# A retention layer with channel mixing: q in packets of two tokens, and the decay moved from the q/k product to v and y

## The chip, the cores and the metric

One core of a Trainium2 chip. The metric is the device time of one execution in microseconds; the profile's "span" (first to last instruction) is about 2 us shorter than the timed run. Executions on a single core are sorted into "fast" and "slow" by their time alone: an execution over 1.5% above the fastest of the same kernel is called slow.

## The reference, cut to what matters

```
# attention: q, k, v are (4 batches, 8 heads, 768 tokens, 64), float32
gamma = 1 - 2 ** (-5 - arange(8))                # one decay per head
state = gamma * state + outer(k[t], v[t])        # per head, 64 x 64
y[t]  = q[t] @ state / 8

# channel mix: x = y with heads side by side, (4, 768, 512)
x_prev = x shifted by one token
xk = mu_k * x + (1 - mu_k) * x_prev ;  xr likewise with mu_r
out = sigmoid(xr @ w_r) * (relu(xk @ w_k) ** 2 @ w_v)     # w_k 512x1024, w_v 1024x512, w_r 512x512
```

## The kernel before

The kernel works on chunks of 128 tokens, 24 in all. Inside a chunk the recurrence is a masked product (k columns by q columns, then by v); between chunks a 64 x 64 state per head is carried. The decay is folded into q and k as they are cast to float16: q gets gamma^u / 8, k gets gamma^-u. A small planner inside the program simulates the engines, orders all tasks, and puts "fillers" (matmuls on a tile of zeros) where it expects TensorE to wait. The parts that the change touches:

```python
# loads: 128 tokens on 128 partitions, 8 heads x 64 values each: packets of 256 bytes
src = s[b, :, c * C : (c + 1) * C, :].rearrange("h t d -> t h d")
nc.sync.dma_start(out=t32.tile[:, n], in_=src)                    # k, q, v in turn
# weights: one transfer into 128 partitions each, rows of 2 KB
wkd = moe_w_k.rearrange("(co ci) f -> ci co f", ci=P)             # w_k in two halves; w_r, w_v alike
# cast of q and k with the decay: VectorE, 24 of them
nc.vector.tensor_tensor(out=qks.tile, in0=t32.tile[:, 0:2],
    in1=Gqk[par].unsqueeze(3).broadcast_to([P, 2, H, D]), op=ALU.mult)
# cast of v: GpSimd or ScalarE
nc.gpsimd.tensor_copy(out=v16.tile, in_=t32.tile[:, 2])
# y leaves PSUM: ScalarE or VectorE
nc.scalar.copy(out=x_out(), in_=y())
... (transposes, masks, state, channel mix, the planner: cut)
```

## Time and profile before

| | before |
|---|---|
| time, median | 181.09 us (4 runs, 180.81 to 181.51), beside the changed kernel |
| span | 178.9 us |
| TensorE / VectorE / ScalarE / GpSimd busy | 167.7 / 150.8 / 102.7 / 29.8 us |
| fillers | 153 |
| second-layer product (w_v) starts | 30.49 us |

The prediction below shows the page and reads it. Three things more are needed for the comparison. First, the page's row of GB/s, in 40 slices of 4.5 us each:

```profile
GB/s 111 223 339 304 253 386 244 222 226 204 255 256 232 200 177 166 136 225 167 199 217 230 191 190 257 194 214 234 31 59 62 0 117 4 59 60 4 117 59 59
```

Second, VectorE's timeline at three casts of weights (start, duration, line, and in brackets how long the engine stood idle and what ended it):

```profile
17.29 1.22 DVE L347 CAST wk<-wk 128x2048 f16<-128x2048 f32 x1
24.54 1.22 DVE L347 CAST wr<-wr 128x2048 f16<-128x2048 f32 x1
30.30 1.23 DVE L347 CAST wv<-wv 128x2048 f16<-128x2048 f32 x1 [2.21 <-DMA wv<-in_moe_w_v_dram]
```

Third, TensorE's timeline at its start:

```profile
1.12 5.07 PE L269 MATMUL pm<-warm 128*128 128x256 f16 x30 [1.12 <-DVE xT L484]
7.18 0.62 PE L398 MATMUL px<-c_sb,qks 128*128 128x128 f16 x8 [0.99 <-DVE qks L385]
7.64 0.71 PE L269 MATMUL pm<-warm 128*128 128x256 f16 x5
```

Thirty fillers in a row take 5.07 us, the first ones at half rate, and by the first transposes TensorE is quick.

### The profile page before, as it was taken

To read this page: it belongs to the slowest core of one execution; us is meant where nothing else is said; L and a number is where in the kernel's file an instruction comes from. 1 tells how busy PE (TensorE), PEld (TensorE's weight loads), DVE (VectorE), ACT (ScalarE), POOL (GpSimd) and SP (SyncE) were. 2 spreads that over 40 slices of the span, in tenths; PEclk is the share of its full clock that TensorE was granted. 3 is DMA by queue.
4 is the path that set the end of the run, shared out by engine and by line. 5 is a ranking of instruction groups with operands and counts; after the bars stand their busy time and mean duration, and the time that the engine had idled before them with its cause. 6 is when DMAs were issued, how large, how long until landed. Compare 5 with 4: busy or idle time off the path is not lost.

```text
span 178.9 us, 4138 instructions
## 1 busy us (share of the span) xinstructions
PE 167.7 (94%) x1698; PEld 113.5 (63%) x1698; DVE 150.8 (84%) x269; ACT 102.7 (57%) x162; POOL 29.8 (17%) x37
## 2 busy tenths in 40 slices
PE   7799899989999799999999999999999999999971
PEld 5678685565877475856757657567666486576450
DVE  0568995988899999999999999999999987999111
ACT  2123565265774866881857936949618458284560
POOL 0030202042130101320131223115213212010000
PEclk9999999999999999999999999999999999999999
DMA  4999999999999878597898889889111030110311
GB/s 111 223 339 304 253 386 244 222 226 204 255 256 232 200 177 166 136 225 167 199 217 230 191 190 257 194 214 234 31 59 62 0 117 4 59 60 4 117 59 59
DMA packets 81298, 30.77 MB, mean 172 GB/s; under 512 B 75512, under 2 KB 75648, under 8 KB 81280
## 3 DMA queue, kind: packets, MB, share of 16 engines
q1 hardware_dynamic: 81280, 30.51, 70.6%
q8 instruction: 13, 0.21, 0.5%
q14 instruction: 5, 0.04, 0.1%
HBM read 24.22 MB, written 6.29 MB: 171 GB/s over the span
## 4 chain that ended last, share of the span: by engine, by line
PE 61%; DVE 14%; SPq 10%; DMA 6%; ACT 3%; issue 3%; POOL 2%; DVEq 0%
PE pm L579 18%; PE pm L543 17%; PE pm L572 9%; SPq L373 6%; DMA wv<-in_moe_w_v_dram 6%; PE px L398 5%; PE px L476 4%; SPq L312 3%; PE pA L413 3%; DVE xr L519 2%; DVE xk L519 2%; DVE a2t L420 2%; PE px L467 2%; DVE osb L590 2%; POOL a2t L427 2%
## 5 line engine op out<-in xcount | busy, mean ns | idle before, releaser
L543 PE MATMUL pm<-xk,wk 128*128 128x128 f16 (+1 forms) x512 | 47.7, 246 | 0.4 <-ACT krel L556 0.4
L579 PE MATMUL pm<-wv,k 128*128 128x512 f16 x192 | 44.9, 379 | 1.0 <-ACT k L562 0.9
L543 PEld LDWEIGHTS <-wk 128*128 128x128 f16 x512 | 39.5, 98 | 5.3 <-issue 0.7
L427 POOL TENSOR_SCALAR_AFFINE_SELECT a2t<-a2t 128x512 f16<-128x512 f16 x24 | 22.1, 920 | 106.5 <-ACT a2t L425 106.5
L385 DVE TENSOR_TENSOR qks<-t,c_sb 128x1024 f16<-128x1024 f32 x24 | 30.0, 1257 | 4.8 <-DMA t<-in_q_dram 4.8
L579 PEld LDWEIGHTS <-k 128*128 128x128 f16 x192 | 18.2, 98 | 21.2 <-ACT k L562 1.4
L556 ACT ACTIVATE krel<-pm 128x512 f32<-128x512 f32 x40 | 23.6, 598 | 13.1 <-PE pm L543 12.7
L425 ACT CAST a2t<-pA 128x512 f16<-128x512 f32 x24 | 14.1, 586 | 22.9 <-DVE a2t L420 22.9
L562 ACT ACTIVATE k<-krel 128x1024 f16<-128x1024 f32 x24 | 25.5, 1061 | 0.4
L519 DVE SCALAR_TENSOR_TENSOR xr<-dx,mu,xT 128x128 f16<-128x128 f32 (+1 forms) x64 | 24.6, 437 | 0.0
L572 PE MATMUL pm<-wr,xr 128*128 128x512 f16 x96 | 24.4, 380 | 0.0
L519 DVE SCALAR_TENSOR_TENSOR xk<-dx,mu,xT 128x128 f16<-128x128 f32 (+1 forms) x64 | 24.3, 431 | 0.1
L491 ACT COPY xT<-px 128x512 f32<-128x512 f32 x24 | 14.1, 586 | 17.6 <-PE px L476 17.6
L590 DVE SCALAR_TENSOR_TENSOR osb<-pm,rsb 128x512 f32<-128x512 f32 x24 | 16.4, 682 | 8.9 <-PE pm L579 8.6
L269 PE MATMUL pm<-warm 128*128 128x256 f16 x153 | 22.5, 288 | 1.4 <-DVE xT L484 1.1
L420 DVE TENSOR_TENSOR a2t<-pA,c_sb 128x512 f16<-128x512 f32 x24 | 16.3, 680 | 1.5 <-PE pA L413 1.5
L269 PEld LDWEIGHTS <-warm 128*128 128x128 f16 x153 | 14.6, 103 | 4.4 <-DVE xT L484 1.1
L511 DVE TENSOR_TENSOR dx<-xT 128x512 f32<-128x512 f32 (+1 forms) x16 | 15.2, 949 | 2.2 <-ACT xT L491 2.1
L454 DVE TENSOR_TENSOR s<-pS,c_sb 128x512 f16<-128x512 f32 x20 | 13.6, 681 | 2.5 <-PE pS L449 1.5
L398 PE MATMUL px<-c_sb,qks 128*128 128x128 f16 x192 | 14.5, 219 | 1.2 <-DVE qks L385 1.2
L391 ACT CAST v<-t 128x512 f16<-128x512 f32 x15 | 9.3, 620 | 10.8 <-DMA t<-in_v_dram 10.8
L476 PE MATMUL px<-a2t,v 128*64 128x128 f16 x192 | 11.7, 225 | 3.5 <-POOL a2t L427 3.5
(29 smaller groups left out, 126.9 us busy)
## 6 DMA issues: line engine op xcount, KB each, us to landing
t<-in_k_dram SPq DMA_DIRECT2D x24, 256.0 KB, 4.3
t<-in_q_dram SPq DMA_DIRECT2D x24, 256.0 KB, 4.9
t<-in_v_dram SPq DMA_DIRECT2D x24, 256.0 KB, 5.0
out_dram<-osb SPq DMA_DIRECT2D x24, 256.0 KB, 2.2
wk<-in_moe_w_k_dram SPq DMA_DIRECT2D x2, 1024.0 KB, 6.6
wv<-in_moe_w_v_dram SPq DMA_DIRECT2D x2, 1024.0 KB
wr<-in_moe_w_r_dram SPq DMA_DIRECT2D x1, 1024.0 KB, 7.4
c_sb<-c SPq DMA_DIRECT2D x1, 64.0 KB, 3.7
```

Of the source, the lines that this page charges most:

```text
L269: nc.tensor.matmul(b.tile[:, 0:256], lhsT=warm[:, 0:P], rhs=warm, start=True, stop=True)
L385: e_qks = add(key, dve(1220, lambda: nc.vector.tensor_tensor(out=qks.tile, in0=t32.tile[:, 0:2], in1=Gqk[par].unsqueeze(3).broadcast_to([P ...
L398: nc.tensor.transpose(o[:, i, j, :], qks.tile[:, i, 2 * j : 2 * j + 2, :], ident)
L420: return dve(690, lambda: nc.vector.tensor_tensor(out=a2t.tile[:, i], in0=pA.tile[:, i], in1=causal4, op=ALU.mult), cost=cost)
L427: e_m1 = add(key + 0.2, pool(700, lambda: nc.gpsimd.affine_select(out=a2t.tile[:, 1], in_=a2t.tile[:, 1], pattern=[[0, NJ], [1, C]], compa ...
L519: nc.vector.scalar_tensor_tensor(out=cut(o)[:, co], in0=cut(dx)[:, co], scalar=mu[:, w * NCO + co : w * NCO + co + 1], in1=prv()[:, co], o ...
L543: nc.tensor.matmul(o[:, n], lhsT=wk16[:, co, fo * P : fo * P + P], rhs=cut(xk)[:, co, :], start=(co == 0), stop=(co == NCO - 1))
L556: act(600, lambda pZ=pZ, o=r_out: nc.scalar.activation(out=o(), in_=pZ.tile, func=AF.Relu, scale=KSC)),
L562: e_sq.append(add(kz + 0.05, act(1060, lambda krel=krel, k2=k2: nc.scalar.activation(out=k2.tile, in_=krel.tile, func=AF.Square)), after=e ...
L572: nc.tensor.matmul(pR.tile, lhsT=cut(xr)[:, co, ts], rhs=wr16[:, co, :], start=(co == 0), stop=(co == NCO - 1))
L579: nc.tensor.matmul(pV.tile, lhsT=o[:, n, ts], rhs=wv16[:, fo, :], start=(fo == 0), stop=(fo == NFO - 1))
L590: 690, lambda pV=pV, rsb=rsb, osb=osb: nc.vector.scalar_tensor_tensor(out=osb.tile, in0=pV.tile, scalar=INV_KSC2, in1=rsb.tile, op0=ALU.mu ...
```

## The change

Its intent: fewer, longer packets for q (two neighbouring tokens of one head lie side by side in memory, 512 bytes), and less work for VectorE. With a pair of tokens in a partition, 64 partitions hold the 128 tokens of one head, so the two halves of the partitions take different heads; heads, query columns and the rows of w_k, w_r and mu are permuted to fit. Since q's partitions no longer hold one token, its decay can't be a number per partition; it moves to y, where it is spread over rows and tokens by two small matmuls at the start (the spread products), and k's moves to v. The q/k cast is then a plain copy. Buffers and the planner's constants are tuned anew, and 12 chunks instead of 8 go through the first layer singly. The core of the diff, with cuts and with the planner's wrappers shortened to the operation and its planned nanoseconds:

```diff
-    src = s[b, :, c * C : (c + 1) * C, :].rearrange("h t d -> t h d")
-    nc.sync.dma_start(out=t32.tile[:, n], in_=src)
+    for g in range(2):                                   # q: two pieces of 64 partitions, 512-byte packets
+        nc.sync.dma_start(
+            out=t32.tile[g * 64 : g * 64 + 64, 0].rearrange("p (h i) d -> p h (i d)", i=2),
+            in_=src.rearrange("(h g) (p i) d -> g p h (i d)", g=2, i=2)[g])
-    wkd = moe_w_k.rearrange("(co ci) f -> ci co f", ci=P)
+    wkd = moe_w_k.rearrange("(a h i e) f -> h i e a f", a=2, h=2, i=2)      # w_r alike
+    for h, i in itertools.product(range(2), range(2)):   # four pieces, 64 partitions each
+        nc.sync.dma_start(out=wide()[h * 64 : h * 64 + 64, i::2], in_=wd[h, i])
-    nc.vector.tensor_tensor(out=qks.tile, in0=t32.tile[:, 0:2], in1=Gqk[par]..., op=ALU.mult)
+    dve(690, nc.vector.tensor_copy(**cast_args())) or act(1010, nc.scalar.copy(**cast_args()))
-    pool(620, nc.gpsimd.tensor_copy(out=v16.tile, in_=t32.tile[:, 2])) or act(600, ...)
+    pool(1000, v_decay(nc.gpsimd)) or dve(690, v_decay(nc.vector))           # v times decay
-    act(590, nc.scalar.copy(out=x_out(), in_=y())) or dve(665, ...)
+    dve(690, nc.vector.tensor_tensor(out=x_out(), in0=y_in(y()), in1=y_in(Gy[:, par]), op=ALU.mult))
+    for par in range(2):                                 # spread the decay of y over rows and tokens
+        nc.tensor.matmul(pG.tile, lhsT=c2[:, 0:P], rhs=c2[:, P + par * 512 : ...])   # 2 rows, float32
... (one float32 buffer of 4 for all weights; dx and xr single; masks, mix and squares on other engines: cut)
```

## The prediction

> **What bounds the kernel now.** I read the page's first two parts, then the work in stretches, then TensorE's timeline, then the chain.
>
> ```profile
> PE 167.7 (94%) x1698; PEld 113.5 (63%) x1698; DVE 150.8 (84%) x269; ACT 102.7 (57%) x162; POOL 29.8 (17%) x37
> ...
> DMA  4999999999999878597898889889111030110311
> ```
>
> TensorE is busy almost throughout, but VectorE is close behind, and the DMA engines are full for the first 60 us. The stretches (TensorE, weight load, VectorE, ScalarE, GpSimd, clock, DMA share, GB/s) show three stages.
>
> ```profile
> 20.00:30.00 10.00, 9.71 (x116) 7.30 (x115) 7.99 (x15) 6.53 (x11) 0.91 (x1) 1.00 1.05 355
> 30.00:40.00 10.00, 9.48 (x97) 6.01 (x96) 9.37 (x17) 3.78 (x6) 1.98 (x2) 1.00 1.01 208
> 50.00:60.00 10.00, 9.73 (x120) 6.91 (x117) 10.00 (x22) 5.81 (x12) 1.54 (x1) 1.00 1.06 241
> 80.00:130.00 50.00, 50.00 (x488) 32.92 (x486) 49.55 (x81) 32.89 (x53) 11.15 (x13) 1.00 0.84 192
> 130.00:170.00 40.00, 39.64 (x367) 25.55 (x366) 33.64 (x67) 22.31 (x35) 5.59 (x6) 1.00 0.15 54
> ```
>
> From 80 to 170 us TensorE has no gap, so nothing is to be had there except fewer columns. Before 60 us the 94% deceives: it holds 153 filler matmuls (on a tile of zeros) that the kernel's planner puts where it expects TensorE to wait.
>
> ```profile
> 28.15 0.24 PE L476 MATMUL px<-a2t,v 128*64 128x128 f16 x1
> 28.63 0.38 PE L476 MATMUL px<-a2t,v 128*64 128x128 f16 x7 [0.24 <-POOL a2t L427]
> 28.95 1.70 PE L269 MATMUL pm<-warm 128*128 128x256 f16 x14
> 30.49 3.84 PE L579 MATMUL pm<-wv,k 128*128 128x512 f16 x16
> ```
>
> Fourteen fillers issue in 30.49 - 28.95 = 1.54 us, 0.11 us each, and the 16 wide matmuls behind them take 3.84 us because they still wait for the last weight cast. The chain gives rates where nothing waits.
>
> ```profile
> 63.71 0.45 PE px L398 x8
> 64.16 1.79 PE pm L543 x32
> ...
> 71.58 0.33 PE pA L413 x8
> ...
> 79.15 3.45 PE pm L579 x16
> ```
>
> So 0.056 us for 128 columns (0.45/8, 1.79/32), 0.042 for the half-array products (0.33/8), 0.216 for 512 columns (3.45/16); the 256-column ones go at 2.62/24 = 0.109 (chain, at 84.93 us). Now add TensorE's in-order list: 296 x 0.216 = 63.9; 256 x 0.109 = 27.9; 608 x 0.056 = 34.0; 384 x 0.042 = 16.1; together 142. The fillers: the first 30 took 5.07 us (slower clock start), the other 123 x 0.11 = 13.5; 18.5. It starts at 1.12. Sum: 161.7 us. The last product issues its last column at about 175 us. **So 13.3 us are waits**, most of them too short to appear as idle. Comparing this running sum with the trace places them: the first transpose is 1.1 us late, the first attention output 1.8, the first wide product (30.49) 4.2, the stretch to 60 us 7.8, 79 us 10.0; the rest lies near the end. The remaining 3.9 us (last product to end of span) is the final gate, store and exit.
>
> **What the Trainium skill says.**
> "DMA: Bandwidth & Descriptors", Why small descriptors are slow: every packet has a fixed overhead. The trace agrees: 256-byte rows move at 208 GB/s with the engines full (30 to 40 us), the stretch with 2 KB weight rows at 355.
> "SBUF — State Buffer", "Can I just issue two DMAs to hit both halves?": a transfer into 64 partitions reaches half the ports, and two such transfers serialize; measured there at 196 GB/s against 328. No transfer of this trace has 64 partitions, so the trace can't say.
> "VectorE: DVE Perf Modes", The perf-mode tier table: a float32 copy in SBUF runs at twice the rate of a tensor_tensor. Agrees: cast of 2048 elements 1218 ns, product of 1024 elements 1257 ns.
>
> ```profile
> L385 DVE TENSOR_TENSOR qks<-t,c_sb 128x1024 f16<-128x1024 f32 x24 | 30.0, 1257 | 4.8 <-DMA t<-in_q_dram 4.8
> L347 DVE CAST wk<-wk 128x2048 f16<-128x2048 f32 x2 | 2.4, 1218 | 0.0
> L427 POOL TENSOR_SCALAR_AFFINE_SELECT a2t<-a2t 128x512 f16<-128x512 f16 x24 | 22.1, 920 | 106.5 <-ACT a2t L425 106.5
> ```
>
> "SBUF — State Buffer", Who interferes with whom: GpSimd and a two-input or fast-mode VectorE instruction lock each other out for a whole instruction. Agrees: the select takes 636 ns at best and 1543 at worst, the q/k product 1204 to 1659.
>
> **The change part by part.** Counts are from the built instruction order of both kernels.
>
> TensorE: 296 wide ones as before; 192 of 256 columns (20.9 us) and 736 of 128 (41.2) in place of 256 and 608, since 12 chunks instead of 8 now go through the first layer alone; half-array 16.1. New: two float32 products that spread the decay, planned at 0.9 us each, before the first transpose. The fillers number 153 again: 19 before those two (3.7 us), 134 x 0.11 = 14.7. Sum: 1.1 + 63.9 + 20.9 + 41.2 + 16.1 + 1.8 + 18.4 = 163.4 us, **1.7 us more** than before. TensorE's own work gives nothing; only the 13.3 us of waits can.
>
> VectorE, sums of single durations (overlap left in on both sides). Before: 162.1 us. After: mix 80 x 0.50 + 32 x 0.37 = 51.8; differences 10 x 1.21 + 4 x 0.68 = 14.8; y times decay 24 x 0.68 = 16.3 (from ScalarE); gates 16.4; masks 18 x 0.68 = 12.2; relu 12 x 0.68 = 8.2; q/k casts 11 x 0.68 = 7.5, against 30.0 for the products; v 9 x 0.68 = 6.1; state 18 x 0.68 = 12.2; weights 6.0; transposed copies 0, against 10.3. Sum 151.5, **10.6 us less**. ScalarE takes 24 transposed copies (24.3 against 9.1) and 13 casts (about 13.8), loses xT and v (23.4): about 18 more on 103 of 179, no bound. GpSimd gets 6 more selects and 15 products instead of 9 casts: 30 x 0.92 + 15 x about 1.2 (estimate: twice the 0.61 of its one-input cast) = 46 us, 1.5 times as many locks; if the excess over the fastest durations (about 7 us now) grows alike, VectorE loses 3 to 4 us of its gain.
>
> DMA: q has 512 packets of 512 B instead of 1024 of 256 B. Per engine 256 KB is 64 packets; at 208 GB/s 1.26 us, 19.7 ns a packet. 2 KB at 355 GB/s is 92 ns. A straight line between gives 30 ns for 512 B: 32 x 30 = 0.96 us, 0.3 us saved per chunk, 1.5 us for the five chunks of the start. The list also puts k and q ahead of the constants (0.4 us earlier) and one chunk more ahead of the last weight. But q and all of w_k and w_r now go in 64-partition pieces.
>
> The start, by the running sum without waits: first transpose 6.6 us (before 7.18, with its wait); first layer's first product 16.4; w_r's product 23.5; second layer's first product 34.3. Data at full rate: before, q of chunk 0 was in at 5.8 us, two loads behind an offset of 3.3; with 1.26 us a load and 2.95 us per MB of weights (355 GB/s) the same sum gives 29.8 us for the last of w_v, and its cast did start at 30.3. After, with offset 2.9 and q at 0.96: w_k's first half 13.1 us, w_r 22.5, the last of w_v 35.4 (it has two more loads of k and v and one of q ahead of it), cast by 36.6. So the second layer waits 36.6 - 34.3 = 2.3 us, against 4.2 of waits up to there before. From there to 80 us, with VectorE lighter, I put 2.5 instead of 5.8, and 3 for the rest, as now. Total 7.8.
>
> **The rivals.**
> A, the above: 163.4 + 7.8 + 3.9 = 175.1 us of span; a timed run is 2.4 longer (181.35 against 178.9): 177.5.
> B, half the ports: w_k and w_r at 196 GB/s need 5.35 us per MB instead of 2.95, and q gains nothing. w_r then lands near 30.6 us, the last of w_v near 44.0, and the second layer waits 45.2 - 34.3 = 10.9 us; VectorE gets ahead meanwhile, so 1 us until 80 and 3 after. Total 14.9: span 182.2, time 184.6. For it: the skill's measurement. Against: 256-byte packets leave engines at half a port's rate anyway, so q at least does not lose, and the kernel's own plan, tuned for this chip, counts q at 0.66 of k.
> C, VectorE's saving is eaten by locks with GpSimd and by single buffers (dx, xr): as A, but 5 us of waits from 34 to 80 and 5 after: 182.0. For it: attention output waited 3.5 us for the select, and selects grow to 30. Against: TensorE had no gap from 80 to 130 us with VectorE full, and VectorE now has slack.
> D, shorter packets simply shorten everything in proportion to DMA time: against it, after 60 us the queue sets nothing.
>
> **Range and chances.** A at 177.5, B at 184.6, C at 182.0; I weigh A at 0.6 and expect mixtures: 179.3 us. Below 175 over two thirds of the waits would have to go (163.4 + 3.9 + 2.4 = 169.7 is the floor without any); above 185.5 B and C would have to add. The 2% line, 177.7, lies just above A: 0.40 faster, 0.50 same, 0.10 slower.
>
> **What would show it.** The unhindered rates and the 163 us sum must hold again: about 153 fillers, the first transpose near 6.6 us. Time from issue to landing of w_k and q tells A from B; a second-layer product that starts near 36 us is A, near 45 is B. VectorE's busy time should fall to about 143 to 147, GpSimd's rise to about 46; more and longer waits of attention outputs for selects would be C. I am wrong altogether if the time goes below 169.7, which the sum forbids, or if gaps open after 80 us.

## The result, and the profile after

| | before | changed |
|---|---|---|
| time, median of 4 | 181.09 us | 190.39 us (190.16 to 190.68) |
| span | 178.9 us | 189.0 us |
| VectorE busy | 150.8 us | 143.5 us |
| GpSimd busy | 29.8 us | 40.6 us |
| second-layer product starts | 30.49 us | 48.30 us |

The ratio is 1.0512, 95% interval 1.0482 to 1.0542: slower, and outside the predicted range. Ratios in this text are the mean time of one kernel's fast runs over that of the other's fast runs of the same rounds, so not quite the ratio of the medians quoted beside them.

The page of the changed kernel, its engines and its row of GB/s (slices of 4.7 us):

```profile
PE 175.6 (93%) x1766; PEld 118.7 (63%) x1766; DVE 143.5 (76%) x252; ACT 112.9 (60%) x159; POOL 40.6 (22%) x52
...
GB/s 115 196 196 203 218 209 201 313 259 241 190 215 182 260 209 238 249 234 244 212 186 237 238 220 200 260 108 111 3 56 59 0 56 59 56 61 56 56 59 57
```

VectorE did get lighter. But where the kernel before moved 253 to 386 GB/s, this one moves 196 to 218 up to 33 us; only slice 8, where w_v comes in one transfer over 128 partitions, jumps to 313. The stretches (columns as in the prediction) say the same, and show what it did to TensorE:

```profile
20.00:30.00 10.00, 7.98 (x107) 6.42 (x105) 5.51 (x12) 3.62 (x6) 1.97 (x4) 1.00 1.06 206
30.00:40.00 10.00, 6.90 (x53) 4.50 (x50) 5.30 (x10) 3.74 (x5) 0.00 (x0) 0.71 1.21 255
80.00:130.00 50.00, 48.82 (x477) 32.22 (x476) 44.31 (x76) 34.55 (x49) 13.59 (x15) 1.00 0.88 209
```

From 20 to 30 us the rate is 206 GB/s against 355 before, at a DMA share of 1.06 against 1.05: the engines are just as "busy" and move little more than half. TensorE is idle for 2.0 of those 10 us and 3.1 of the next 10, and in that second stretch its granted clock falls to 0.71. VectorE works 5.5 us where it worked 8.0: it starves. After 80 us TensorE is nearly full; two gaps, 0.78 us before 99.73 us and 0.28 us before 106.30, are most of the 1.2 us that it idles there, where the kernel before had none. So most of the loss is at the start. VectorE's timeline at the same casts as above:

```profile
27.14 1.23 DVE L398 CAST wk<-w 128x2048 f16<-128x2048 f32 x1 [2.46 <-DMA w<-in_moe_w_k_dram]
32.25 1.23 DVE L398 CAST wr<-w 128x2048 f16<-128x2048 f32 x1 [3.29 <-DMA w<-in_moe_w_r_dram]
46.69 1.22 DVE L398 CAST wv<-w 128x2048 f16<-128x2048 f32 x1
```

Now the second half of w_k and w_r are what VectorE waits for; their casts come 9.9 and 7.7 us later than before. TensorE's timeline shows the waits behind them:

```profile
28.43 1.07 PE L649 MATMUL pm<-xk,wk 128*128 128x128 f16 x16 [2.02 <-DVE wk L398]
...
33.54 1.33 PE L681 MATMUL pm<-wr,xr 128*128 128x512 f16 x4 [2.39 <-DVE wr L398]
...
36.01 1.04 PE L473 MATMUL px<-c_sb,qks 128*128 128x128 f16 x8 [0.71 <-ACT qks L455]
```

The last line is a transpose that waited for a q of a later chunk; its eight products take 1.04 us, at half rate after the idle time. The chain of waits names both culprits in two consecutive links, from issue to landing:

```profile
17.86 7.89 DMA w<-in_moe_w_k_dram
25.77 8.99 DMA t<-in_q_dram
```

Placed against the prediction's running sum: the second layer would start at 34.3 us without waits and starts at 48.30, so 14.0 us of waits (time at half rate among them) lie before it, against 4.2 in the kernel before.

At the very start there is something else:

```profile
1.12 4.23 PE L284 MATMUL pm<-warm 128*128 128x256 f16 x19 [1.12 <-DVE xT L578]
5.28 3.78 PE L371 MATMUL pm<-c_sb 2*128 2x512 f32 x4
8.99 1.03 PE L473 MATMUL px<-c_sb,qks 128*128 128x128 f16 x8
9.82 1.70 PE L284 MATMUL pm<-warm 128*128 128x256 f16 x7
```

All 19 fillers run at half rate, the spread products take 3.78 us, and what follows is still slow (eight transposes in 1.03 us instead of 0.62, seven fillers in 1.70).

### The profile page after: what moved, and what is told of

It reads as the page before. It is cut to its first block, busy times and chain, and to the rows that moved or that the text cites. A ratio compares the mean times of both kernels' runs of the same rounds, so it can differ in the third digit from the quotient of the medians.

```text
span 189.0 us, 4352 instructions
## 1 busy us (share of the span) xinstructions
PE 175.6 (93%) x1766; PEld 118.7 (63%) x1766; DVE 143.5 (76%) x252; ACT 112.9 (60%) x159; POOL 40.6 (22%) x52
## 4 chain that ended last, share of the span: by engine, by line
PE 51%; DMA 19%; SPq 11%; issue 5%; ACT 5%; DVE 5%; POOL 1%; ACTq 0%; POOLq 0%; DVEq 0%
PE pm L649 15%; PE pm L688 15%; PE pm L681 7%; DMA t<-in_q_dram 7%; SPq L427 6%; DMA t<-in_v_dram 5%; DMA w<-in_moe_w_k_dram 4%; PE px L473 3%; PE pm L284 3%; SPq L432 2%; PE pA L495 2%; PE px L569 2%; SPq L394 2%; DMA t<-in_k_dram 2%; ACT qks L455 2%
## 5 line engine op out<-in xcount | busy, mean ns | idle before, releaser
L649 PEld LDWEIGHTS <-wk 128*128 128x128 f16 x576 | 40.6, 99 | 7.4 <-DVE wk L398 2.3
L483 ACT COPY qkT<-px 128x1024 f16<-128x1024 f16 x24 | 24.0, 1012 | 14.1 <-PE px L473 14.0
L506 ACT CAST a2t<-pA 128x512 f16<-128x512 f32 x30 | 17.0, 587 | 17.1 <-PE pA L495 12.3
L618 DVE SCALAR_TENSOR_TENSOR xk<-dx,mu,xT 128x256 f16<-128x256 f32 (+1 forms) x56 | 26.8, 520 | 0.2
L284 PE MATMUL pm<-warm 128*128 128x256 f16 x153 | 25.6, 312 | 1.1 <-DVE xT L578 1.1
L618 DVE SCALAR_TENSOR_TENSOR xr<-dx,mu,xT 128x256 f16<-128x256 f32 (+1 forms) x56 | 24.8, 478 | 1.2 <-PE pm L681 1.0
L460 POOL TENSOR_TENSOR v<-t,c_sb 128x512 f16<-128x512 f32 x15 | 16.5, 1102 | 26.3 <-PE px L569 15.7
L455 ACT CAST qks<-t 128x1024 f16<-128x1024 f32 x13 | 13.7, 1051 | 7.3 <-DVE dx L609 3.7
L588 DVE TENSOR_TENSOR xT<-px,Gy 128x512 f32<-128x512 f32 x24 | 16.2, 684 | 1.3 <-PE px L569 1.0
L504 DVE TENSOR_TENSOR a2t<-pA,c_sb 128x512 f16<-128x512 f32 x18 | 12.4, 688 | 5.7 <-ACT a2t L506 4.4
L694 ACT ACTIVATE rsb<-pm 128x512 f32<-128x512 f32 x24 | 13.8, 599 | 3.8 <-PE pm L681 3.5
```

What stands on the lines that cost most here:

```text
L284: nc.tensor.matmul(b.tile[:, 0:256], lhsT=warm[:, 0:P], rhs=warm, start=True, stop=True)
L455: act(1010, lambda: nc.scalar.copy(**cast_args()), cost=COST["qk"])],
L483: act(1010, lambda: nc.scalar.copy(out=qkT_out(), in_=pT.tile.bitcast(F16))),
L506: act(590, lambda: nc.scalar.copy(out=a2t.tile[:, i], in_=pA.tile[:, i]), last=False, cost=COST["mask"])], after=after, takes=takes, uses= ...
L618: (200 + TM) / 0.96, lambda w=w, o=o, co=co: nc.vector.scalar_tensor_tensor(out=cut(o)[:, co], in0=cut(dx)[:, co], scalar=mu[:, w * NCO + ...
L649: nc.tensor.matmul(o[:, n], lhsT=wk16[:, co, fo * P : fo * P + P], rhs=cut(xk)[:, co, t0 : t0 + TM], start=(co == 0), stop=(co == NCO - 1))
```

## The experiments

Three theories to begin with. **P**: a transfer into 64 neighbouring partitions gets half the ports, so w_k, w_r and q come slowly (the prediction's rival B). **G**: the float32 spread products hold up TensorE's start and everything behind it. **L**: GpSimd's locks and the single buffers slow VectorE (rival C). In the table, "before" is the median of the kernel before in the same rounds on the same chip. "Wrong" means that the result is wrong, because the data lands in other rows; instructions, bytes and order are the same.

| run | edit | result | time, us (all runs) | before | ratio |
|---|---|---|---|---|---|
| w_whole | w_k, w_r over 128 partitions | wrong | 183.85 (182.25–185.06) | 181.57 | 1.006 |
| q_whole | q over 128 partitions | wrong | 186.75 (185.64–187.68) | 181.57 | 1.028 |
| gy_f16 | spread in float16 | correct | 190.88 (189.86–191.01) | 181.57 | 1.049 |
| before_w_halves | kernel before, w_k, w_r in halves | correct | 187.41 (187.03–187.72) | 181.57 | 1.031 |
| both_whole | w_whole and q_whole | wrong | 179.58 (177.67–181.53) | 181.64 | 0.980 |
| decay_only | natural layout, decay on v and y | correct | 182.35 (181.25–183.29) | 181.64 | 1.005 |
| decay_f16 | the same, spread in float16 | correct | 181.70 (180.37–182.49) | 181.64 | 1.001 |
| before_q_512 | kernel before, q in 512-byte packets | wrong | 181.30 (180.32–181.56) | 181.64 | 0.998 |
| w_pieces | w_k, w_r in 4 pieces over 128 partitions | wrong | 184.14 (182.86–185.37) | 181.45 | 1.014 |
| q_inter | q's pieces on even and odd partitions | correct | 187.39 (186.75–188.33) | 181.45 | 1.033 |
| ports_all | all loads over all ports | correct | 179.36 (178.17–182.35) | 181.45 | 0.985 |
| ports_all_f16 | the same, spread in float16 | correct | 179.47 (178.72–181.28) | 181.45 | 0.991 |
| ports_all_b | ports_all again | correct | 181.27 (179.39–182.47) | 181.43 | 0.991 |
| ports_late_f16 | float16 spread behind the transpose | correct | 182.27 (182.03–183.12) | 181.43 | 1.005 |
| ports_pad | float16 spread, padded to 128 rows | correct | 180.22 (179.46–180.64) | 181.43 | 0.992 |

The times are medians over all runs; slow ones are among those of w_whole (one of four), both_whole (two of four), ports_all (two of six) and ports_all_b (three of six), whose fast runs alone average 183.3, 177.8, 178.9 and 179.7 us. For both_whole the ratio is worked out from its two fast runs: (177.67 + 177.97) / 2 over 181.48, the mean of before there.

### Whole transfers in the changed kernel: w_whole and q_whole

```diff
-    wkd = moe_w_k.rearrange("(a h i e) f -> h i e a f", a=2, h=2, i=2)
+    wkd = moe_w_k.rearrange("(co ci) f -> ci co f", ci=P)             # w_whole; w_r alike
```

> The changed kernel with w_k and w_r loaded as before, each half in one transfer over 128 partitions (the result is wrong on purpose: feature rows in natural order). Theory P, half the ports: the change loses its time because 64-partition pieces move at about 200 GB/s, so 3 MB of weights arrive up to 7 us late; here the rate while weights flow returns to over 300 GB/s, w_r's cast starts near 26 us instead of 32.3, and the time falls by 4 to 7 us, to 184 to 186. Rival G, the float32 spread products at the start (3.8 us instead of the planned 1.8, and a slow TensorE clock after them) cost most of it: then the time falls by under 2 us. Rival L, locks and steady-state waits: under 1 us.

```diff
-    for g in range(2): nc.sync.dma_start(out=t32.tile[g * 64 : g * 64 + 64, 0]..., in_=...[g])
+    two = q[b, c % 2 * 4 : c % 2 * 4 + 4, c // 2 * 2 * C : c // 2 * 2 * C + 2 * C, :]
+    nc.sync.dma_start(out=t32.tile[:, 0].rearrange("p (h i) d -> p h (i d)", i=2),
+                      in_=two.rearrange("h (p i) d -> p h (i d)", i=2))        # q_whole
```

> The changed kernel with q's 512-byte rows in one transfer over 128 partitions (same bytes and packets; the result is wrong on purpose, half the heads of two chunks). Theory P: q too is held to half the ports, one piece pair takes about 1.3 us instead of the 0.96 predicted; four to five chunks of it in the start make 1.2 to 1.8 us, so 188.5 to 189.5. If packets and not ports set q's rate: unchanged, 190.4. If P is much stronger for q than for the weights: below 187.

Measured: 6.5 us of the 9.3 us lost come back with whole weights, 3.6 us with whole q. From 20 to 30 us w_whole moves 293 GB/s and its second layer starts at 40.15 us; in q_whole it is 44.08. P holds for the weights. For q it holds more strongly than the 188.5 to 189.5 us that I had expected: the halves did cost q something, though its packets are short. q's own rate can't be read there: from 20 to 30 us q_whole moves 207 GB/s, like the changed kernel, since its weights still come in halves.

### The reverse: before_w_halves

```diff
-    dma_start(out=w32, in_=wd)
+    for h in range(2):
+        r = slice(h * 64, h * 64 + 64)
+        dma_start(out=w32[r], in_=wd[r])        # w_k and w_r only, in the kernel before
```

> The kernel before with only this of the change: w_k and w_r in pieces of 64 partitions (result right). Theory P: 3 MB at half rate delay the last weight by about 7 us (its cast from 30.3 to 36 or 37 us) and the time rises by 4 to 6 us, to 185.5 to 187. Rivals G and L: under 1 us.

Measured: +5.8 us on a kernel that is otherwise untouched, and correct. Its stretches and its second w_k cast:

```profile
20.00:30.00 10.00, 7.40 (x89) 6.34 (x89) 7.00 (x17) 3.35 (x5) 0.00 (x0) 0.83 1.04 226
```

```profile
22.37 1.23 DVE L352 CAST wk<-wk 128x2048 f16<-128x2048 f32 x1 [3.83 <-DMA wk<-in_moe_w_k_dram]
```

226 GB/s instead of 355, and the cast at 22.37 instead of 17.29, after 3.83 us of waiting for its data; the last w_v cast comes at 36.44, as expected. One line of the change, transplanted, reproduces the symptom.

### The spread products: gy_f16

```diff
-    c2 = const_pool.tile([2, c2_np.shape[1]], F32, name="c2_sb")
+    c2 = const_pool.tile([2, c2_np.shape[1]], F16, name="c2_sb")
```

> The changed kernel with the two spread products in float16 instead of float32, same instruction order otherwise (still right within the tolerance). Rival G: the first transpose starts near 6.5 to 7 us instead of 9.0 and the clock is up by 9 us instead of 13.5; if the start hangs on TensorE's list, the time falls by 3 to 5 us. Theory P: the first chunk is early but the weights are late all the same (w_r's cast still near 32 us), so the time falls by less than 1 us.

Measured: 190.88, nothing gained, although the first transpose now starts at 6.75 us instead of 8.99. (Not all of that need be the edit: with float32 products and the same start, the profiled executions of w_pieces and q_inter have it at 6.59 and 7.25.) The second half of w_k still is not cast before 28.25. G falls as the cause: 2.2 us saved at the start are waited away at the weights.

### Both parts whole: both_whole

The two edits of w_whole and q_whole together.

> The changed kernel with w_k, w_r and q all loaded by transfers that write 128 partitions; q still in 512-byte packets (other tokens and heads than it should have, so the result is wrong on purpose), every other instruction and the order the same. Theory P (the 64-partition pieces are the whole loss, and all pieces stand in one queue): the two gains measured singly, 6.5 and 3.6 us, add up: 190.4 - 10.1 = 180.3 us, 179.3 to 181.5; second layer's first product near 48.3 - 8.2 - 4.2 = 36 us. Rival S (after the first gain another limit takes over, the late spread products or locks between VectorE and GpSimd): less than 7.5 us of the 10.1, 183 us or more. Prediction's A, without any cost that it left out: 177.5.

Measured: two runs at 177.7 and 178.0, two at 181.2 and 181.5, all at a granted clock of 0.995 or more. The median, 179.58, is within the additive range but lies between the two groups; the fast pair is 1.5 us below that range. There was no sign of a next limit in the profiled (fast) run, whose stretch, w_r cast and first second-layer product read:

```profile
20.00:30.00 10.00, 9.88 (x128) 7.44 (x126) 8.01 (x14) 6.24 (x9) 1.91 (x3) 1.00 1.12 296
```

```profile
23.33 1.23 DVE L398 CAST wr<-w 128x2048 f16<-128x2048 f32 x1 [0.54 <-DMA w<-in_moe_w_r_dram]
```

```profile
36.72 1.89 PE L688 MATMUL pm<-wv,k 128*128 128x512 f16 x8
```

The prediction's version A had w_r in at 22.5 us, the second layer at 36.6, a span of 175.1 and a time of 177.5. This run has 23.3, 36.72, a span of 176.0 and 177.67 us. So in the fast executions the sum for everything but the ports was right within 1 us; the slow pair is 3.5 us longer, and the prediction foresaw no second group. L falls with it: GpSimd, buffers and order here are those of the changed kernel.

### How many pieces, or how many ports: w_pieces and q_inter

Whole transfers are also fewer transfers. Two controls keep their number and change only where they land.

```diff
-    for h, i in product(range(2), range(2)): dma_start(out=wide()[h * 64 : h * 64 + 64, i::2], in_=wd[h, i])
+    for o in range(4): dma_start(out=wide()[:, o], in_=wd[:, o])               # w_pieces
```

> A control for the number of transfers: the changed kernel with w_k and w_r in four pieces of 256 KB each, as the change has them, but each piece writes 128 partitions instead of 64 (natural rows, result wrong on purpose). Theory P (half the ports): as the run with whole weight transfers, 183.9 us, 182.2 to 185.1, and about 290 GB/s from 20 to 30 us. Theory N (it was the number of transfers, their issue and their small size, that cost): as the changed kernel, 190.4, and 206 GB/s.

```diff
-    out=t32.tile[g * 64 : g * 64 + 64, 0]...      qkT.tile[r, 0, 2 * a : 2 * a + 2, g * 64 : g * 64 + 64]
+    out=t32.tile[g::2, 0]...                      qkT.tile[r, 0, 2 * a : 2 * a + 2, g::2]      # q_inter
```

> The changed kernel, correct, with q's two pieces of 64 partitions written to the even and to the odd partitions instead of the lower and the upper half; TensorE takes the query columns at stride 2 to undo it. Same packets, same number of transfers. Theory P: each piece now reaches every port: 186.75 as with q whole, 185.6 to 187.7. If any transfer of 64 partitions is slow, however they lie, or if the count of transfers is it: 190.4. If the strided columns slow TensorE, its query products get longer than 0.042 and 0.056 us each and it is above that.

Measured: w_pieces 184.14, as w_whole (183.85), with

```profile
20.00:30.00 10.00, 8.57 (x107) 6.47 (x105) 6.98 (x12) 5.88 (x9) 1.66 (x2) 1.00 1.13 312
```

So the number of pieces costs nothing that can be seen in runs that are 2.5 us apart among themselves. q_inter is at 187.39, 3.0 of q_whole's 3.6 us, with the same two transfers of 64 partitions each, merely interleaved. For q, then, it is not the count of partitions that costs the time but that the 64 are neighbours. Weights in interleaved pieces were not tried. TensorE takes columns at stride 2 without loss: in both_whole and q_inter alike the eight masked products take 0.40 us when TensorE is at full rate.

### What each half of the change is worth: decay_only, decay_f16, before_q_512

```diff
-    return 4 * (j // 2) + 2 * hp + j % 2          # head(j, hp)
+    return 2 * j + hp                             # decay_only: natural heads, tokens, rows; q loaded as k and v (cut)
```

> The changed kernel with the natural layout of heads, tokens and features, correct: q loaded as k and v are (256-byte packets, 128 partitions, one transfer), w_k, w_r and mu whole; the decay still on v and y, GpSimd, buffers and order as changed. If 512-byte packets are worth the 0.3 us per chunk that I estimated, this is 1.5 us slower up to the last weight than the kernel with both whole: 181 to 182.5 us. If packets of 512 B over all ports are worth more (1 us a chunk), 184 or more. If they are worth nothing, the two are equal.

> The same with the decay spread by float16 products, correct. In the changed kernel this was worth nothing (190.9) though the first transpose came 2.2 us earlier, because the loads set the start. If the loads with all ports still set the start: equal to decay_only within 0.7 us. If the late first transpose now sets it: 1 to 2 us faster, 179.5 to 181.

```diff
+    if i == 1: src = two.rearrange("h (p i) d -> p h (i d)", i=2)      # before_q_512: q alone, over 128 partitions; two as in q_whole
```

> The kernel before with q alone in 512-byte packets into 128 partitions (other tokens, result wrong on purpose). What the changed loads were meant to bring, without the 64 partitions: with my estimate of 0.3 us a chunk the last weight is in 0.9 to 1.2 us earlier, 180.0 to 181.0 us; if 512-byte packets need the same time per byte, no change: 181.3.

Measured: moving the decay alone gains nothing (182.35, ratio interval 0.9994 to 1.0100): the lighter VectorE waits for the last weight instead, which stands behind two chunks more in the queue and whose cast starts at 38.42 us, having waited 0.98 us. With 512-byte packets over all ports (both_whole) that cast starts at 35.26 without a wait: 3.2 us earlier over five chunks, 0.6 us a chunk rather than my 0.3 (an estimate, since the layout of the cast differs as well). In the kernel before the same packets bring the last w_v cast from 30.30 to 29.79, 0.17 us for each of the three chunks ahead of it, and the time down by 0.3 us, with an interval (0.9944 to 1.0019) that includes nothing at all; the 180.0 to 181.0 us that I expected did not come. So what the packets save, 0.17 or 0.6 us a chunk, stays open. The float16 spread is worth 0.65 us in medians here; with this scatter that is not settled.

### A correct version over all ports: ports_all, ports_all_f16

Natural heads, so that w_k, w_r and mu load whole; q in 512-byte packets into even and odd partitions; the cast of k straight and of q permuted, in two instructions.

```diff
+    out=t32.tile[g::2, 0]..., in_=src.rearrange("(g h) (p i) d -> g p h (i d)", g=2, i=2)[g]
+    copy(out=qks.tile[:, 1], in_=t32.tile[:, 1])
+    copy(out=qks.tile[:, 0].rearrange("p (a i h) d -> p a i h d", a=2, i=2),
+         in_=t32.tile[:, 0].rearrange("p (a h i) d -> p a i h d", a=2, i=2))
```

> A correct version of the change with every transfer over all ports: heads paired naturally, so w_k, w_r and mu load as before; q in 512-byte packets into even and odd partitions; the cast of q and k in two instructions (k straight, q permuted). Theory P: as the wrong-on-purpose kernel with both whole (177.7 to 181.5, median 179.6) plus at most 1 us for 24 more cast instructions: 178 to 181.5, median 180, which is about 0.8% below before. If q's two pieces still cost: 183 or more.

> The same with the decay spread by float16 products. It was worth nothing in the changed kernel (loads set the start) and 0.65 us in the natural layout; with the loads quicker I expect 0.5 to 1.5 us below the kernel without it: 178 to 180, median 179, a version that beats both kernels by a little over 1% against before. If the first transpose is not on the path: equal.

Measured: ports_all 179.36 us, fast runs 0.9853 of before (0.9819 to 0.9887); two of its six runs, at 182.2 and 182.4, count as slow. ports_all_f16 is at 179.47 and, against my expectation, does not beat it by the fast runs (over all six runs of each it averages 179.7 against 180.0).

### Why two groups: ports_all_b, ports_late_f16, ports_pad

The granted clock was 1.0 in the upper group as well. **W**: the two-row spread products interrupt TensorE's start, and in some executions it then stays at half rate until about 13.5 us. **X**: something else, memory for instance.

> The version with every transfer over all ports once more, to stand on the same chip beside the two that follow. Its executions fell into two groups, 178.2 to 179.7 and 182.2 to 182.4, at the same granted clock; I expect both groups again. Theory W (the float32 spread products over 2 rows interrupt the start of TensorE, which then stays at half its rate until about 13.5 us): the profiled execution shows spread products of 3.8 us when it is of the upper group, about 2 us when it is of the lower.

```diff
-    spread products before the first transpose           # ports_late_f16: after it; the planner re-orders
+    after=[k_c2, e_T]
```

> The same, correct, with the spread products in float16 and moved behind the first transpose, so that 34 fillers stand unbroken before it (the planner then orders the rest a little otherwise, 177 fillers in all). Theory W: TensorE is at its full rate before the first transpose in every execution, the upper group is gone: all runs between 178 and 180, median 178.8. Rival X (the groups come from something else, memory for instance): the upper group, 181 and above, stays in about a third of the runs. 27 more fillers may cost up to 3 us where the plan put them in a wait that doesn't come; then all runs are later, but in one group.

```diff
+    c2 = const_pool.tile([P, c2_np.shape[1]], F16, name="c2_sb")       # ports_pad
+    nc.gpsimd.memset(c2, 0.0)                                          # rows 2 to 127 stay zero
```

> The version with float16 spread products in the old place, with the two rows padded by zero rows to 128, so that these two products fill the array's rows; order as in the version with all ports. If it is the two-row shape that keeps TensorE slow: no run above 180.5, the first transpose's neighbours at 0.056 and 0.11 us in the profile. If it is the length of the unbroken start instead: as ports_all_f16, 178.7 to 181.3, and the seven fillers after the first transpose again take 1.7 us in a slow one.

Measured: ports_all_b has both groups again, 179.4 to 180.2 and 182.3 to 182.5, three runs each. Its profiled execution is one of the lower group, with spread products of 1.98 us; the profiled execution of ports_all was one of the upper, with 3.78 us, its first w_k cast at 18.03 instead of 16.04 and its second layer at 40.08 instead of 38.09. That is as W had it, by one profile of each, and accounts for 2.0 of the 3 us between the groups. In ports_pad all six runs lie between 179.46 and 180.64, one group, and its start reads:

```profile
5.14 1.06 PE L370 MATMUL pm<-c_sb 128*128 128x512 f16 x2
6.50 0.62 PE L471 MATMUL px<-c_sb,qks 128*128 128x128 f16 x8 [0.29 <-DVE qks L448]
6.96 0.93 PE L286 MATMUL pm<-warm 128*128 128x256 f16 x7
```

TensorE is quick from the first transpose on. In ports_all_f16, with the same order and two-row float16 products, the seven fillers took 1.70 us in the profiled run. That the two rows are the cause is likely but not shown. The kept traces speak for it: of the twelve profiled executions with two-row products before the first transpose, five were at half rate until 10 to 14 us (the changed kernel, w_whole, q_whole, ports_all, ports_all_f16) and three fell back to it from about 9 to 12 us (gy_f16, q_inter, ports_all_b), while the five without (before, before_w_halves, before_q_512, ports_late_f16, ports_pad) were quick by about 6.5 us and stayed so to 14. But four with two rows (w_pieces, both_whole, decay_only, decay_f16) were quick too, so one profile of ports_pad doesn't decide. Nor does a slow start alone make the upper group: that profiled run of ports_all_f16 took 178.93 us, and none of its six runs is in that group (the highest is 181.28), so float16 may have removed it as well as the padding. X stays untested. ports_late_f16 lost its upper group too, but all its runs are at 182 to 183, a miss: its second layer starts at 38.73, about where ports_all_b has it (38.09), and the rest is lost later, in an order that the planner made anew. I did not follow that, and as its one group sits where the upper group was, it says nothing for or against W.

Over all twelve runs ports_all averages 180.5 us and ports_pad, over six, 180.1: either is ahead of both kernels, by 0.5 to 0.8% against before (less than the 2% that the prediction counts as faster) and over 5% against the changed one. By its fast runs alone ports_all is 0.9 to 1.5% ahead of before.

## Why the prediction was wrong

- **The step that failed is "Data at full rate"**: the landing times of w_k, w_r and w_v (13.1, 22.5, 35.4 us) were worked out at 355 GB/s for pieces that write 64 neighbouring partitions, and A, which rests on it, was weighed at 0.6. Rates of 196 to 218 GB/s in the trace, and w_pieces, q_inter and before_w_halves, show that such pieces go at little more than half. Rival B named this, with the figure; I set against it two arguments that don't carry. "256-byte packets leave engines at half a port's rate anyway" was read from the old packets (208 GB/s against 355), while q's new ones were 512 bytes, and q in halves lost 3.6 us. "The kernel's own plan counts q at 0.66 of k" is a constant that somebody typed; nothing says that it was measured on this layout.
- **B itself was too mild**: it had w_r in by 30.6, the second layer at 45.2 and a span of 182.2; measured were 32.25, 48.30 and 189.0. Of the 3.1 us at the second layer, q's own loss, which B put at nothing, is enough (q_whole moves the second layer by 48.30 - 44.08 = 4.2 us). After the second layer B allowed 4 us of waits; the running sum gives 189.0 - 163.4 - 3.9 - 14.0 = 7.7. Part of this rest is q's again: from the first second-layer product to the end of the span w_whole and w_pieces, with q in halves, took 142.1 and 141.7 us, and both_whole, with the same instructions and q whole, 139.3. The remainder no run splits.
- **"The first transpose near 6.6 us"** came at 8.99: the term "planned at 0.9 us each" for the spread products measured 3.78 us together, not 1.8, in that execution; in others with the same start it was 1.98 to 2.24 us and the transpose came at 6.59 to 7.46 (w_pieces, q_inter, both_whole). Here it was hidden (gy_f16 gained nothing); with all ports it goes with the 3 us between the two groups.
- **The TensorE sum of 163.4 us** held: 153 fillers as counted, and both_whole's span of 176.0 leaves 176.0 - 163.4 - 3.9 = 8.7 us of waits, where the prediction had 7.8.
- **VectorE** at 143.5 us is in the predicted 143 to 147. GpSimd at 40.6 is below 46: its selects averaged 766 ns, not the 920 of before; the v products, 1102 ns, were near the estimated 1.2 us.
- **C (locks)** did not come: both_whole has all of C's ingredients and meets A. The sign "if gaps open after 80 us" did come (0.78 and 0.28 us in the changed kernel), but it did not mean that the account was wrong altogether: they are small beside the loss at the start.
- **"From there to 80 us, with VectorE lighter, I put 2.5 instead of 5.8"** was right in direction: the running lag grows by 1.4 us between 48.30 and 75.6 us in the changed kernel. That is over 27 us, though, against 49 us in the kernel before. The fairer check is both_whole, where by the same sum the lag grows by 2.3 us from 36.72 to 80 us; so the gain in the middle came, but that the lighter VectorE made it is not shown by itself. In the changed kernel the start lost 9.8 us more than before and buried it.
- **Slips in the working**, none of which decided the result: "one chunk more ahead of the last weight" is two, as the queue has five chunks before the last of w_v where it had three (the sum for 35.4 us counts all five). ScalarE's listed terms add up to 24.3 - 9.1 + 13.8 - 23.4 = 5.6 us more, not 18; measured were 10.2. The profiled execution of the kernel before took 180.83 us, so a timed run is 1.9 us longer than the span, not 2.4, and A would be 177.0. To go below 175, 8.0 of the 13.3 us of waits would have to go, 60% and not over two thirds. "1.5 times as many locks" is 45 GpSimd instructions for 33, 1.4 times. From 80 to 170 us TensorE does have one gap, 0.36 us before 135.20. And the 196 and 328 GB/s stand under Door 1 of the page, not in the section that the prediction names.

## What to carry to other kernels

When a transfer is cut for a layout, look at which partitions each piece writes, not only at its packet size and number: here pieces of 64 neighbouring partitions cost about 10 us, while q in 64 interleaved ones, or weights in four pieces over all 128, cost next to nothing. A DMA share near 1 doesn't mean that data flows; read the GB/s beside it. And when a rival in a prediction comes with a measured figure, an argument from a constant in the program should not outweigh it.

## What the Trainium skill lacked or had wrong

- "SBUF — State Buffer", Door 1: The DMA port swizzle, with "Can I just issue two DMAs to hit both halves?": the 196 GB/s for 64 partitions is what this queue showed (196 to 218 GB/s in a mix with other loads, against 253 to 386 before), and the page's 328 for 128 partitions is near 293 to 355 in the stretches with whole weights. Its sentence that "the only way to hit all 16 ports is one transfer spanning all 128 partitions" is too strong: two transfers to the even and to the odd partitions (q_inter) won back 3.0 of 3.6 us (read from the times, not from a rate). The page's own mapping from partition to port would allow it; no example says so.
- "TensorE: Matmul & The Clock Gate", What's actually happening, has a start at half rate of some 3.4 us of sustained matmuls. The kernel before agrees: of 30 fillers in 5.07 us some 16 were slow, 3.5 us (an estimate, at 0.22 and 0.11 us each). The same 30 took 4.76 us in before_q_512 and 5.89 in before_w_halves. The page has nothing on whether matmuls over 2 rows count as such. These runs raise the question and don't settle it: with two-row products before the first transpose, eight of twelve profiled executions were slow there or fell back (seven fillers in 1.70 us at 9.82 in the changed kernel), with none there or with padded ones none of five (0.93 us at 6.96 in ports_pad).
- No page that I used has this case: the granted-clock row of a profile does not show this start. It read 1.00 from 0 to 10 us in the changed kernel, where fillers took 0.22 us instead of 0.11. The later fall it does show (0.50 from 9 to 12 us in q_inter).
